# Five batches with the gates' exponential a step sooner and the first scatter a step later, and each following batch's v loaded a pair later

## The chip, the cores and the metric

The kernel runs on one core of one Trainium2 chip. The metric is device time in microseconds (us). The kernel before has a median of 724.61 us over three runs (723.22, 724.61, 727.99).

## The reference

Block-causal attention over q, k and v of shape (8, 8, 576, 64) (batch, head, position, width; blocks of 64 positions), and then a top-1 mixture of eight experts on the 4608 rows of 512 that the attention gives:

```python
scores = scale * np.matmul(q, k.transpose(0, 1, 3, 2))      # masked where block_i < block_j
attn = softmax(scores);  x = np.matmul(attn, v)             # -> (4608, 512)
logits = x @ w_gate;  e_idx = np.argmax(logits, axis=1)
gate_w = softmax(logits)[rows, e_idx]
eom = 1.0 / (1.0 + np.exp(-(x @ w_output_gate)))
out[mask] = gate_w[mask, None] * eom[mask, e, None] * (np.maximum(x[mask] @ w1[e], 0.0) @ w2[e])
```

## The kernel before

The work of the attention goes by batch (8) and by pair of heads (4 in a batch), so there are 32 pairs, p = 0 to 31, b = p // 4. TensorE's (PE's) instructions stand in the order in which the code writes them (`manual_schedule`); on the other engines and on SP's queue a planner sets the order from the order of the code and its own costs, within the edges that `issue_after` adds (`behind()`: after the last chained instruction on POOL; `queued()`: after the last transposing DMA).

`attend` (line 1210 on) writes one pair as a string of letters. For most pairs it is `S.F.SVuFSV.FttSF<t.`; `S` is a step of the softmax of pair p (`softmax`: scores, maximum, exponential, for row tiles 0 and 1, 2, 3, and last the 64 rows that remain), `F` a step that transposes the probabilities of pair p - 1 (`flip`), `V` a half of the values of pair p - 2 (`values`), `t` a step of the generators in `later`, `<` starts `finish_batch`, and a dot calls `others(r)` with r = 0, 1, 2, 3. From p = 26 a pair has four `t`.

`others` prepares inputs. `split_qk` makes 16-bit high and low parts of q and k on POOL (lines 151, 156, 158) for a pair some three ahead. `turn_qk` (line 167) sends one transposing DMA on SP's queue that turns them into the tile `qk` of a pair: 28 of these, for pairs 4 to 31 in order; pairs 0 to 3 are turned on PE. In the first eight pairs it is written at most one pair ahead of its use, later two. `fetch` loads q and k of a later batch (lines 117, 123, 111). `load_v` (lines 336, 338) loads v of the next batch in three DMAs, 512, 512 and 128 KB, one per call of `others`; it starts at the third pair of a batch (`hp == 2`). Tile `vv` has two buffers. `own_keys(b, m)` (line 347) copies parts of v into `vd0` (two buffers) and `vd1` (one) on POOL, which `values` reads from pair 4b on, that is, while p = 4b + 2 is written.

`finish_batch(b)` (line 555 on) starts at the end of p = 4b + 5 and makes the gate's logits, the row numbers and the scatter into the table of rows. For batches 0 to 4 (`slow`) it is cut into some 26 steps of `t`. The steps that matter here: in step 12 the sums of the hot row, `se` and `zs`, on VectorE (DVE, lines 700 to 717); step 13 transposes and scales the last rows of the attention (`part_rows(LAST)`, lines 537, 540); step 14 sends these rows out and has ScalarE (ACT) do the exponential of the gates `zs` (line 724), behind the last softmax exponential written; steps 15 and 16 are small operations on POOL (line 629); step 17 the reciprocal on DVE (line 740); from step 18 on, five scatters on POOL (line 752), two steps apart. The finished rows go to DRAM by SP (line 552).

After the attention come the experts (lines 1128 and 1163), from some 340 us on; nothing there is touched.

Of the kernel before, what the change touches and what calls it, by code (L numbers as in the profile page):

```python
# [26 lines left out]
def block_attention_top1_moe(  # L27
# [12 lines left out]
    B, H, S, D = q.shape  # L40
    NTOK, DM = out.shape
    E, _, FF = w1.shape
    NP = H // 2
# [4 lines left out]
    LAST = NT - 1  # L48
# [92 lines left out]
    def queued():  # L141
        return tc.issue_after(last_turn[0].ins) if last_turn[0] else nullcontext()
# [20 lines left out]
    def turn_qk(p):  # L163

        sp = halves.pop(p)
        qk = sb.tile([P, 2, NB * P], F16, name="qk", bufs=3)
        last_turn[0] = nc.sync.dma_start_transpose(
            qk.rearrange("c h (r n) -> c (h r) n", n=P), sp.rearrange("p h n a d -> p (h n a d)")
        )
        loaded[p] = qk  # L170
# [158 lines left out]
    def load_v(b):  # L329

        vv = sb.tile([P, H, LAST, D], F32, name="vv")
        vd = [None, None]
        vl = vlast[b % 2]
        values_of[b] = vv, vd, vl
        for m in range(2):
            nc.sync.dma_start(vv[:, :, 2 * m:2 * m + 2].rearrange("p h i d -> p h (i d)"), couples(v, b, m))
            yield
        nc.sync.dma_start(vl[0:64], pair_of(v[b, :, S0:S]))
        yield

    def own_keys(b, m):

        vv, vd, vl = values_of[b]
        vd[m] = sb.tile([P, H, D], F32, name=f"vd{m}", bufs=2 - m)
        for i in range(2):
            with behind():
                last_pool[0] = nc.gpsimd.tensor_copy(vd[m][64 * i:64 * i + 64], vv[0:64, :, 2 * m + i])
# [180 lines left out]
    def finish_batch(b, sums, sumL, xT):  # L528
# [3 lines left out]
        def rows(t):  # L532

            r = ROWS[t]
            pm = ps_t.tile([P, 512], F32, name="ps_t")
            for g in range(NP):
                nc.tensor.transpose(pm[0:r, P * g:P * g + P], xT[:, g, Q0[t]:Q0[t] + r], ident)
            xn = sbx.tile([P, DM], F32, name="xn", bufs=NT - 1)
            with tc.high_priority(offset=5):
                last_row[0] = nc.vector.tensor_tensor(  # L540
                    xn[0:r].rearrange("p (h d) -> p h d", d=D), pm[0:r].rearrange("p (h d) -> p h d", d=D),
                    rec[0:r, t].unsqueeze(2).broadcast_to([r, H, D]), ALU.mult,
                )
            held.append((x_d[b * S + Q0[t]:b * S + Q0[t] + r, :], xn[0:r]))
            if rush:
                store()

        def store():

            while held:  # L550
                with queued() if not rush else nullcontext():
                    nc.sync.dma_start(*held.pop())
# [13 lines left out]
        held, rush, mid, slow = [], b == B - 1, b == B - 3, b < B - 3  # L566
# [66 lines left out]
        def after(last):  # L633
            return tc.issue_after(last[0].ins) if pool else nullcontext()

        def part(n):

            for x in range(n if slow else 0):
                yield

        def part_rows(*ts):

            for t in ts:
                rows(t)
                yield
                store()
# [70 lines left out]
            nc.vector.tensor_reduce(zs, z, AX.X, ALU.add)  # L717
        if slow:
            yield
            yield from part_rows(LAST)  # L720
        if mid:
            yield
        with after(last_exp) if pool or rush else tc.issue_after(last_flip[0].ins):
            last_gate[0] = nc.scalar.activation(zs, zs, AF.Exp, scale=-1.0)
        yield from part(1)
        if slow:
            on_pool(
# [10 lines left out]
        yield from part(1)  # L738
        with after(last_max):
            nc.vector.reciprocal(idg.bitcast(F32)[:, b, :, 1], zs)  # L740
        yield from part(1)
        if mid:
            rows(2)
        for t in range(NT):
            r = ROWS[t]
# [261 lines left out]
    def load_first():  # L1007

        route_first()
        for j in range(2):  # L1010
            with behind():
                last_pool[0] = nc.gpsimd.memset(xg[j], 0.0)
        with behind():
            fetch_ids(steps[0])
        fetch_ids(steps[1], (0, 1))
        last_pool[0] = read[0]
        with chain():
            ev = nc.sync.value_load(f_i[0:1, 0:1], min_val=0, max_val=E - 1)

        wc = {}  # L1020

        def load(w, c):
            dt, nm = ((F16, "hh"), (BF16, "hl"))[c % 2]
            wc[c] = fs.tile([P, KF, 2, P], dt, name=nm).rearrange("p f h n -> p (f h n)").bitcast(F32)
            nc.sync.dma_start(quarter(w, wc[c]), rows_of(w, ev, c))

        for c in range(4):
            load(w1, c)
        with behind():
            read[0] = nc.gpsimd.tensor_copy(w1b[0][:, 0, 0], wc[0].rearrange("p (g m) -> p g m", g=KF))  # L1030
        with tc.issue_after(read[0].ins):
            fetch_x(steps[0])
        fetch_x(steps[1], (0, 1))
        for r in range(5):
            yield
        for c in (1, 0, 2, 3):
            if c:
                with tc.issue_after(last_exp[0].ins):
                    nc.scalar.copy(w1b[0][:, 0, c], wc[c].rearrange("p (g m) -> p g m", g=KF))
            for g in range(0, KF, 4):  # L1040
                with tc.issue_after({1: last_max, 0: last_row, 2: last_xT, 3: last_low}[c][0].ins):
                    nc.vector.tensor_tensor(
                        w1b[0][:, 1, c, g:g + 4].bitcast(BF16), wc[c].rearrange("p (g m) -> p g m", g=KF)[:, g:g + 4],
                        w1b[0][:, 0, c, g:g + 4], ALU.subtract,
                    )
            load(w2, c)
            for r in range((1, 3, 1, 0)[c]):
                yield
        first_w2.extend(wc[c] for c in range(4))
# [160 lines left out]
    def step(g, n=1):  # L1210
        for i in range(n):
            next(g, None)
# [45 lines left out]
    for p in range(NPR):  # L1258
        b, hp = divmod(p, NP)
        if hp == 0:  # L1260
            sums = small.tile([P, NT, H], F32, name="sums", bufs=3), small.tile([P, NP], F32, name="sumL", bufs=3)
            nc.gpsimd.memset(sums[0][64:128, LAST, :], 1.0)
            xT = sbx.tile([P, NP, S], F32, name="xT")
        if p == NPR - 2:
            ld.release()
            wp = ctx.enter_context(tc.tile_pool(name="wp", bufs=1, side="right"))
            fs = ctx.enter_context(tc.tile_pool(name="fs", bufs=2, side="right"))
            w1b.append(wp.tile([P, 2, KD, KF, P], F16, name="w1b0"))
            w2b.append(wp.tile([P, 2, KF, DM], F16, name="w2b0"))
            for j in range(2):  # L1270
                xg.append(wp.tile([P, 2, DM], F32, name=f"xg{j}"))
            later.append(load_first())
        if p == 0:
            fetching.append(load_v(0))
        if b + 1 < B and hp == 2:
            fetching.append(load_v(b + 1))
        early = turn_first(p + 1) if p + 1 < NP else None

        def others(r):
            if early is not None:  # L1280
                step(early)
            if r % 2 == 0 and qk_next[0] in halves and qk_next[0] <= p + 1 + (p >= SURE):
                turn_qk(qk_next[0])
                qk_next[0] += 1
            if not splits and splitted[0] < min(NPR, p + 3 + (p >= SURE)):
                splits.append(split_qk(splitted[0]))
                splitted[0] += 1
            for g in list(splits):
                if next(g, splits) is splits:
                    splits.remove(g)  # L1290
            for m in range(2):
                if (p, r) == ((max(1, NP * b), 1), (NP * b + 1, 2))[m]:
                    own_keys(b, m)
            nb = fetched[0] + 1
            free = splitted[0] - len(splits) >= NP * (nb - 1) and p >= NP * (nb - 2) + 1
            if nb < B and not r % 2 and (p == 0 and nb == 1 or (p, r) == (2, 2) and nb == 2 or nb > 2 and free):
                fetching.append(fetch(nb))
                fetched[0] = nb
            with queued():
                for g in list(fetching):  # L1300
                    if next(g, fetching) is fetching:
                        fetching.remove(g)

        probs = {}
        attend(softmax(p, *sums, probs), others)
        flips.append((hp, b, probs, sums, xT, values_of[b]))
        if p == CP:
            with tc.issue_after(last_max[0].ins):
                constants()
# [23 lines left out]
    hp, b, pT, vab, sums, xT = prods.pop()  # L1333
# [155 lines left out]
```

## Time and profile before

| | |
|---|---|
| median of three runs | 724.61 us |
| profiled execution | 724.29 us |
| its span, first to last instruction | 722.7 us |
| PE busy | 695.7 us (96%) |
| DVE, ACT, POOL busy | 540.7, 498.5, 336.6 us |
| DMA queue that SP feeds, share of 16 engines | 70.2% |

A timeline row gives the start and the length of a run of equal instructions, the engine, the line, the operation with its tiles and shapes, the count, and in brackets how long the engine stood idle before it and what ended that. SPq is SP's DMA queue: the length there is that of issuing, not of the transfer. The engine's idle time before an instruction is put down to the releaser that came last by the profile; where that one had long been done, it was another.

### The profile page before, as it was taken

Reading aid. Unit: us, or ns where it says so; the run is one execution under the profiler, and the core shown is the slowest. Engines: PE = TensorE matmul, PEld = TensorE weight load, DVE = VectorE, ACT = ScalarE, POOL = GpSimd, SP = SyncE. Lnnn points to the kernel's source line nnn. Section 1 sums busy time; section 2 is a strip of 40 time slices with the busy share of each in tenths; the row PEclk is TensorE's granted clock in tenths of the full one; section 3 lists DMA queues with packets and bytes.
Section 4 is the critical chain, followed back from the end, with each engine's and each line's share of the span. In section 5 each row is a group of like instructions: output and inputs, shape, how many; then the busy total and the mean of one; then the engine's idle time right before and its main releaser. Section 6 shows DMA issues by size and latency. Waiting matters only on the chain. (4 is left out here: it accounts for less than half of the span.)

```text
span 722.7 us, 21738 instructions
## 1 busy us (share of the span) xinstructions
PE 695.7 (96%) x8604; PEld 508.8 (70%) x8604; DVE 540.7 (75%) x947; ACT 498.5 (69%) x1096; POOL 336.6 (47%) x447
## 2 busy tenths in 40 slices
PE   8999999999999998998999999999999999999994
PEld 6677877777777776677577758677586676757761
DVE  6878988898988896796887658667586687858730
ACT  6889887788888885772476667566675777757630
POOL 4575688778787776315456314222143134211011
PEclk9999999999999999999999999999999999999997
DMA  7999499999899864479376886947999999777611
GB/s 191 273 200 249 94 236 157 211 198 213 175 187 200 158 128 66 162 228 240 88 135 171 262 281 159 265 144 210 301 308 291 333 339 300 261 228 168 241 37 41
DMA packets 218847, 146.88 MB, mean 203 GB/s; under 512 B 153584, under 2 KB 186416, under 8 KB 218736
## 3 DMA queue, kind: packets, MB, share of 16 engines
q1 hardware_dynamic: 209984, 125.85, 70.2%
q0 software_dynamic: 8208, 19.29, 9.3%
q8 instruction: 69, 1.13, 0.7%
q14 instruction: 42, 0.34, 0.2%
q10 hardware_dynamic: 544, 0.26, 0.1%
HBM read 126.43 MB, written 19.34 MB: 202 GB/s over the span
## 5 line engine op out<-in xcount | busy, mean ns | idle before, releaser
L1128 PEld LDWEIGHTS <-w1b 128*128 128x128 f16 (+1 forms) x2208 | 176.7, 98 | 21.9 <-issue 1.7
L1128 PE MATMUL ps_s<-xt,w1b 128*128 128x256 f16 (+5 forms) x1920 | 174.8, 253 | 0.0
L1163 PE MATMUL ps_t<-w2b,hh 128*128 128x512 f16 (+1 forms) x560 | 166.6, 379 | 0.0
L992 DVE TENSOR_TENSOR w2b<-w2f,w2b 128x1024 bf16<-128x1024 f32 x80 | 92.8, 1220 | 87.1 <-ACT w2b L990 85.0
L395 DVE TENSOR_REDUCE nmx<-ps_s 128x1 f32<-128x512 f32 (+4 forms) x224 | 130.0, 616 | 23.2 <-PE ps_s L384 8.9
L388 ACT ACTIVATE pt<-ps_s,nmx 128x256 f32<-128x256 f32 (+3 forms) x256 | 132.2, 532 | 5.9 <-DVE nmx L395 4.6
L1171 POOL DMA_INDIRECT out_dram<-ys,ids x38 | 45.5, 1199 | 169.2 <-ACT ys L1170 85.9
L1163 PE MATMUL ps_t<-w2b,hl 128*128 128x512 f16 x280 | 106.1, 379 | 0.0
L1170 ACT ACTIVATE ys<-ps_t,ids 128x512 f32<-128x512 f32 (+1 forms) x38 | 26.0, 685 | 105.6 <-PE ps_t L1163 76.5
L1163 PEld LDWEIGHTS <-hh 128*128 128x128 f16 x560 | 54.4, 98 | 61.8
L992 DVE TENSOR_TENSOR w1b<-w1f,w1b 128x1024 bf16<-128x1024 f32 x80 | 93.2, 1218 | 5.4 <-ACT w1b L990 5.1
L990 ACT CAST w1b<-w1f 128x1024 f16<-128x1024 f32 x80 | 78.4, 1045 | 8.4 <-DMA w1f<-in_moe_w_dram 8.4
L505 PE MATMUL ps_t<-pT,vv 128*64 128x128 f32 (+1 forms) x512 | 80.1, 392 | 0.0
L990 ACT CAST w2b<-w2f 128x1024 f16<-128x1024 f32 x80 | 77.8, 1043 | 0.9 <-DMA w2f<-in_moe_w_dram 0.8
L375 PE MATMUL ps_s<-qk 64*128 64x256 f16 (+1 forms) x1152 | 72.5, 253 | 4.1 <-ACT pt L388 1.9
L468 DVE COPY pT<-ps_f 128x512 f32<-128x512 f32 x93 | 63.5, 683 | 17.1 <-PE ps_f L465 13.2
L959 POOL DMA_INDIRECT xg<-x_d,ids x38 | 54.8, 1442 | 31.7 <-DVE w1b L992 9.4
L468 ACT COPY pT<-ps_f 128x512 f32<-128x512 f32 x93 | 55.2, 594 | 14.2 <-PE ps_f L465 11.4
L375 PEld LDWEIGHTS <-qk 64*128 64x128 f16 x1152 | 48.4, 95 | 17.0 <-issue 12.0
L752 POOL DMA_INDIRECT tab_d<-idg,sli x40 | 41.4, 1034 | 34.8 <-DVE idg L740 13.6
L465 PEld LDWEIGHTS ps_f<-ident,pt 64*128 64x128 f32 x1116 | 42.3, 138 | 21.3 <-issue 15.3
L1136 ACT ACTIVATE hh<-ps_s 128x1024 f16<-128x1024 f32 (+2 forms) x46 | 38.9, 846 | 26.2 <-PE ps_s L1128 24.1
(228 smaller groups left out, 1113.9 us busy)
## 6 DMA issues: line engine op xcount, KB each, us to landing
w1f<-in_moe_w_dram SPq DMA_DIRECT2D x80, 512.0 KB
w2f<-in_moe_w_dram SPq DMA_DIRECT2D x80, 512.0 KB
vv<-in_v_dram SPq DMA_DIRECT2D x16, 512.0 KB
x_d<-xn SPq DMA_DIRECT2D x32, 256.0 KB
natk<-in_k_dram SPq DMA_DIRECT2D x14, 512.0 KB
natq<-in_q_dram SPq DMA_DIRECT2D x28, 256.0 KB
hh<-in_moe_w_dram SPq DMA_DIRECT2D x4, 512.0 KB
hl<-in_moe_w_dram SPq DMA_DIRECT2D x4, 512.0 KB
```

The source lines that it names most:

```text
L375: nc.tensor.matmul(ps[:, ab, c:c + m], qk[rows, cq, P * t:P * t + P], cols(qk[rows, ck], x, kind), start=(i == 0), stop=(i == 2 and c + m ...
L388: last_exp[0] = nc.scalar.activation(probs[t][:, ab], ps[:, ab, c0:c0 + n], AF.Exp, bias=nmx[:, t, ab:ab + 1], accum_out=sums[:, t, 2 * hp ...
L395: last_max[0] = nc.vector.tensor_reduce(o, x, AX.X, ALU.max, negate=True)
L465: nc.tensor.transpose(ps[:, h, 64 * i:64 * i + 64], src[rows], ident[rows, rows])
L468: copy(to[:, h], ps[:, h].rearrange("p (s c) -> p s c", c=P))
L505: nc.tensor.matmul(pa[o, P * t0:P * t1].rearrange("p (t h n) -> p t h n", h=2, n=64), vd[j // 2][:, a0 + ab] if t1 == j + 1 and j % 2 == 0 ...
L959: nc.gpsimd.indirect_dma_start(out=xg[i % NXG][:, h], out_offset=None, in_=x_d[0:nx, :], in_offset=IOA(ap=ids[i][:, h, 0:1].bitcast(U32), ...
L990: nc.scalar.copy(hi, src)
L992: eng.tensor_tensor(lo, src, hi, ALU.subtract)
L1128: nc.tensor.matmul(ph[:, f4].rearrange("p (h n) -> p h n", n=w), wv[:, cc, f, :], xv[:, cc, :, 0:w], start=(k == 0), stop=(k == 3 * KD - 1))
L1163: nc.tensor.matmul(py, hv[:, f, h], wv[:, f, :], start=(k == 0), stop=(k == 3 * KF - 1))
L1171: nc.gpsimd.indirect_dma_start(out=out, out_offset=IOA(ap=ids[i][0:r, h, 0:1].bitcast(U32), axis=0), in_=ys[0:r], in_offset=None, bounds_c ...
```

## The change

Four edits. In `finish_batch`, for the slow batches, `part_rows(LAST)` moves behind the exponential of the gates, so that the exponential is written in step 13, ahead of the last rows, instead of in step 14. The wait between the reciprocal and the first scatter becomes two steps instead of one for the slow batches, so the five scatters are written a step later each. `load_v(b + 1)` starts at the fourth pair of a batch instead of the third. And `own_keys(b, 0)` is written at p = 4b + 1, r = 0, instead of p = 4b, r = 1, for b > 0.

```diff
@@ finish_batch
         if slow:
             yield
-            yield from part_rows(LAST)
         if mid:
             yield
         with after(last_exp) if pool or rush else tc.issue_after(last_flip[0].ins):
             last_gate[0] = nc.scalar.activation(zs, zs, AF.Exp, scale=-1.0)
+        if slow:
+            yield from part_rows(LAST)
         yield from part(1)
@@
         with after(last_max):
             nc.vector.reciprocal(idg.bitcast(F32)[:, b, :, 1], zs)
-        yield from part(1)
+        yield from part(2)
         if mid:
             rows(2)
@@ the loop over pairs
-        if b + 1 < B and hp == 2:
+        if b + 1 < B and hp == NP - 1:
             fetching.append(load_v(b + 1))
@@ others
             for m in range(2):
-                if (p, r) == ((max(1, NP * b), 1), (NP * b + 1, 2))[m]:
+                if (p, r) == ((NP * b + 1, 0 if b else 1), (NP * b + 1, 2))[m]:
                     own_keys(b, m)
```

## Rows read from the trace of the kernel before

**Rows 1.** The page's part 1, PE's line: busy us, share, instructions.

```profile
PE 695.7 (96%) x8604; PEld 508.8 (70%) x8604; DVE 540.7 (75%) x947; ACT 498.5 (69%) x1096; POOL 336.6 (47%) x447
```

**Rows 2.** Windows: PE, PEld, DVE, ACT, POOL busy (instructions), granted clock, DMA share, GB/s.

```profile
120.00:140.00 20.00, 18.88 (x333) 14.48 (x330) 16.28 (x38) 15.34 (x50) 15.99 (x26) 1.00 1.04 200
160.00:180.00 20.00, 19.97 (x359) 15.32 (x357) 16.72 (x39) 16.76 (x54) 16.25 (x30) 1.00 0.93 204
```

**Rows 3.** Timeline of PE and its weight loads: starts of pairs 5, 13, 14, the values, a transpose.

```profile
49.62 0.34 PE L375 MATMUL ps_s<-qk 64*128 64x128 f16 x6 [0.19 <-ACT pt L388]
122.72 0.34 PE L375 MATMUL ps_s<-qk 64*128 64x128 f16 x6 [1.10 <-ACT d L676]
...
122.72 0.17 PEld L375 LDWEIGHTS <-qk 64*128 64x128 f16 x6 [1.33 <-DMA qk<-sp]
...
132.53 0.34 PE L375 MATMUL ps_s<-qk 64*128 64x128 f16 x5
...
134.93 0.39 PE L505 MATMUL ps_t<-pT,vd 128*64 128x128 f32 x4
...
141.65 0.66 PE L596 MATMUL ps_t<-ident,lgT 128*128 128x128 f32 x4 [0.24 <-ACT lgT L564]
```

**Rows 4.** Timeline of SP's queue, third batch into the fourth.

```profile
98.75 3.02 SPq L336 DMA_DIRECT2D vv<-in_v_dram  x2
...
108.14 0.73 SPq L338 DMA_DIRECT2D vlast<-in_v_dram  x1
...
111.28 3.56 SPq L167 DMA_TRANSPOSE qk<-sp  x1
...
116.99 5.52 SPq L167 DMA_TRANSPOSE qk<-sp  x1
```

**Rows 5.** Timeline of ACT around line 724, two batches, and DVE's reciprocal.

```profile
102.34 0.23 ACT L724 ACTIVATE zs<-zs 128x5 f32<-128x5 f32 x1
102.45 0.60 ACT L564 COPY lgT<-ps_t 128x512 f32<-128x512 f32 x1
...
133.87 0.59 ACT L468 COPY pT<-ps_f 128x512 f32<-128x512 f32 x1 [0.65 <-PE ps_f L465]
...
133.25 0.40 DVE L590 RECIPROCAL rec<-rec 128x40 f32<-128x40 f32 x1 [0.41 <-ACT rec L585]
```

**Rows 6.** Timeline of POOL: copies of v, the gates' steps, a first scatter.

```profile
128.15 1.27 POOL L347 COPY vd<-vv 64x512 f32<-64x512 f32 x2 [0.16 <-PE ps_t L505]
...
141.27 0.23 POOL L629 TENSOR_SCALAR zs<-zs 128x5 f32<-128x5 f32 x1 [3.64 <-ACT zs L724]
...
149.41 1.06 POOL L752 DMA_INDIRECT tab_d<-idg,sli  x1 [2.71 <-DVE xT L523]
```

**Rows 7.** Timeline of SP's queue, first batch into the second.

```profile
26.88 1.25 SPq L336 DMA_DIRECT2D vv<-in_v_dram  x2
28.17 2.42 SPq L338 DMA_DIRECT2D vlast<-in_v_dram  x1
...
41.65 4.11 SPq L167 DMA_TRANSPOSE qk<-sp  x1
```

**Rows 8.** Timeline of PE, POOL and SP around pair 29.

```profile
261.54 0.92 PE L435 MATMUL ps_s<-qk,qlast 128*128 128x256 f16 x9
270.68 0.90 PE L435 MATMUL ps_s<-qk,qlast 128*128 128x256 f16 x9
...
282.48 0.22 PE L519 MATMUL ps_t<-pT,vv 128*64 128x64 f32 x1 [1.63 <-issue]
...
284.24 1.62 PE L435 MATMUL ps_s<-qk,qlast 128*128 128x256 f16 x9
...
270.87 1.27 POOL L347 COPY vd<-vv 64x512 f32<-64x512 f32 x2
...
274.08 2.93 SPq L167 DMA_TRANSPOSE qk<-sp  x1
```

**Rows 9.** Windows around pair 29, columns as in rows 2.

```profile
282.00:288.00 6.00, 5.01 (x67) 3.77 (x66) 3.30 (x6) 3.64 (x9) 3.91 (x5) 0.72 0.01 2
```

## The prediction

> **What bounds it now.** I read the page first, for the share of each engine [rows 1], then windows over the attention to see in which stretches PE is idle [rows 2], then the timeline of PE there [rows 3], and for each gap the queue or engine that ended it [rows 4 to 9]. PE is busy for 695.7 of 722.7 us [rows 1], and no other engine comes near. In an undisturbed stretch of the attention it is idle for 0.03 us in 20; in the stretch from 120 to 140 for 1.12 [rows 2]. So the change, which takes no work off PE, can only win back single gaps. I find three that it touches.
>
> The largest in the regular part of the attention is that of 1.10 us ahead of the first scores of pair 13 at 122.72. The row of PE names ACT, but the weight load of the same step waited 1.33 us for the transposed tile [rows 3]: the transposing DMA of pair 13, the tenth of the 28, issued from 111.28 to 114.84, landed nearly 8 us after its issue ended. Ahead of it on SP's queue stand the three DMAs of v of the batch [rows 4]. The second gap is 0.24 us at 141.65, where PE waits for ACT's copy of the logits [rows 3], and the gates' exponential stands right ahead of that copy on ACT, 0.23 us long [rows 5]. The third is in pair 29: from its predecessor's last softmax step to its own pass 13.56 us, against 9.14 for the pair before that [rows 8].
>
> **The parts.** *v a pair later.* What moves is three issues per batch for seven batches, 3.02 + 0.73 us on SP in the batch shown [rows 4], and 1,152 KB; at the 200 to 204 GB/s of the stretches [rows 2] that is some 5.8 us of the DMA engines. They come to stand behind the transposing DMA that is written in the fourth pair of a batch, instead of ahead of it; in the batch shown that is pair 13's, which so goes out some 3.75 us sooner with 5.8 us less in front; it needs 1.33. Bounds: from 0 (the lateness came from something else in the queue) to 1.33; I take the 1.10 that PE stood idle.
>
> The same v now stands ahead of the next transposing DMA, pair 14's: issued from 116.99 to 122.51 [rows 4], used at 132.53 [rows 3], so 10.0 us are there between the end of the issue and the use. At the 7.9 us that pair 13's took, 2.1 are spare, and an undisturbed queue leaves more. I take 0 for it, since the 7.9 us were seen with v in front and at a DMA share of 1.04 and above, and the shares of the other batches are lower [rows 2]; the other end is in the rivals.
>
> In the first batch the distance is shorter, as a pair's transposing DMA is there written one pair ahead only. Pair 5's is issued from 41.65 to 45.76 [rows 7] and used at 49.62, and PE did not wait for it (its 0.19 us went to ACT) [rows 3]: at most 3.86 us are spare. The v of batch 1, 1.25 + 2.42 us of issue from 26.88 on [rows 7], moves from ahead of pair 4's transposing DMA to between pair 4's and pair 5's. It stood ahead of pair 5's before too, so only what the queue cannot fill in its place is lost. Bounds: 0, if the loads of q and k close the hole, and 5.8 if none of it is filled and nothing was spare; I take 0.3, near the low end, since 3.86 of the 5.8 may be covered.
>
> *The copy of v on POOL.* The same 1.27 us [rows 6], a pair later. Its reader is the value product two pairs into the batch: the second copy, at 128.15 and done at 129.42 [rows 6], stays where it is, the first now stands just before it, and the first product that reads either is at 134.93 [rows 3]. That leaves 5.5 us, so 0. If v had not landed, POOL would stand with the splits of q and k behind it; but from its issue to the copy there are still some two pairs of about 9.14 us [rows 8], against 5.8 of transfer. `vv` has two buffers, and the load comes later than before, so it waits for no release.
>
> *The exponential a step sooner.* It takes 0.23 us of ACT away from ahead of the logits' copy [rows 5], five times: between 0 and 5 x 0.24 = 1.2 us; I take 0.24, since of the five batches one shows PE waiting there. It then stands behind the last softmax exponential one pair earlier, where ACT stood idle for 0.65 us soon after [rows 5], which covers it; but the sums' copy for the next batch comes behind it, and DVE already waits 0.41 us for that ahead of the next maximum [rows 5]. Bounds: 0 to 5 x 0.23 = 1.15; I take 0.2. On POOL the wait of 3.64 us for the exponential goes [rows 6], and what is late next is the first scatter: it waits 2.71 us for DVE's reciprocal (the row names another DVE instruction) [rows 6] and will wait that much longer. POOL's splits come sooner, and PE waits for none of them. So 0.
>
> *The last rows behind it.* The transposes on PE and the scaling stay in the same step and in their order among PE's instructions; their DMA is in step 14 as before. 0.
>
> *The scatters a step later.* Five issues on POOL, about 1.06 us each [rows 6], per slow batch. Nothing before the experts reads the table, POOL is busy for 16 of 20 us [rows 2], and the splits that they are moved past serve pairs two and more ahead: 0, and at most 1.06 us once if a split came to be late.
>
> *Pair 29.* Its PE gap has rows like 1.63 us with "issue" as releaser: PE waited for nothing that the profile shows [rows 8]. Behind it the granted clock is 0.72 over 6 us [rows 9], that is, in part at 1.2 instead of 2.4 GHz, and a softmax step takes 1.62 us instead of 0.90 [rows 8]. Just ahead of it, the transposing DMA of pair 31 leaves at 274.08, when POOL has split its q and k, and the copy of v that the change moves stood in that split for 1.27 us [rows 8]. So that DMA would leave 1.3 us sooner against PE's work. Whether this moves the gap no row tells: the bounds are a gain of 13.56 - 9.14 = 4.4 and 1.7 us of clock (0.28 of 6 us [rows 9]), and a loss of 1.3. I take 0.
>
> **The sum.** 724.29 (the profiled execution, 1.6 us around its span and 0.3 below the median of 724.61) - 1.1 - 0.24 + 0.2 + 0.3 = 723.45, so 723.4 us.
>
> A rule speaks for no gain from moving loads around a transposing DMA. In the rows the DMA share is 0.93 to 1.04 while 200 to 204 GB/s are moved [rows 2]. The Trainium skill (Advanced Engine Details and Errata, X-Bar Transpose (TRN2)) says that transposing DMAs are as fast as regular ones, and gives 350 to 400 GB/s; with so fast a queue nothing would be late behind 1,152 KB, and the time would be the third rival's. The trace does not agree: its engines are taken up at about half that rate.
>
> **Rivals.** *First, the gap of pair 29 goes too* with the earlier transposing DMA: 723.45 - 4.4 - 1.7 = 717.4, and in part anything up to 721.5. For it: the DMA share falls to 0.01 just after [rows 9], so something that was in flight then ended the stall. Against: most of what surrounds it (stores, scatters of a batch that the change leaves alone) stays. Chance 0.2.
>
> *Second, slower: the transposing DMA behind v comes late.* v's 5.8 us beat the 2.1 us that are spare at pair 14's, and so for pairs 10, 18, 22, 26 and 30, and for pair 5. A late one costs up to 3.7 us; priced like the one that the trace shows, 1.10, all seven make 723.15 + 7.7 = 730.9, and half of them 727. It decides where such a DMA lands more than 10.0 us after its issue. For it: DMA shares around 1 [rows 2]. Against: v left the queue ahead of it by as much. Chance 0.13.
>
> *Third, nothing to measure:* pair 13's was late because its own transfer was slow, and stays late, or another takes its place. 724.3 to 725. For it: among 28 only one was waited for, though all batches load v alike. Chance 0.17.
>
> **The numbers.** The forecast, 723.4 with 721.5 to 724.3 of its own, has 0.5. The range of 718.0 to 727.5 leaves out the lower end of the first rival and, of the second, the case that more than half are late. One per cent, about what a measurement of this kernel can tell from no change, is 7.2 us: under 717.4 needs all of the first rival and more (0.07), over 731.9 the second at nearly its worst (0.04), and 0.89 is between.
>
> **What would show it.** Right: the weight load at pair 13 waits for no transposed tile; v's DMAs stand behind the transposing DMA written in the fourth pair of a batch on SP; POOL no longer waits for the gates' exponential, and waits longer for the reciprocal ahead of the first scatter; the step ahead of the logits' transposes is free of waits. Wrong: weight loads wait for transposed tiles at pairs 5, 10, 14, 18, 22; PE is idle for longer around pair 29, or not at all; a new wait of DVE's maximum for ACT at the start of a batch.

## The result, and the profile after

The changed kernel takes 732.45 us in the median of 19 runs (726.18 to 736.45), the kernel before 725.94 us in as many beside it: 1.0091 times as long, 95% interval 1.0071 to 1.0111. Such ratios, here and below, leave out executions in a slower state of the chip (in e2 two of six) and can differ by some tenths of a per cent from the quotient of the medians shown. The forecast was 723.4 us, about 1 us less than before, with a range to 727.5; the change is slower by some 6.5 us, and the time lies outside the range. The profiled execution took 733.86 us, its span is 732.2 against 722.7 us.

Where the 9.5 us of span went is read from the start of the last softmax step (line 435) of each pair, in both timelines:

| stretch | before | after | difference |
|---|---|---|---|
| start to pair 0 | 13.60 | 14.52 | +0.92 |
| pair 5 | 8.07 | 9.61 | +1.54 |
| pair 13 | 10.10 | 8.94 | -1.16 |
| pair 15 | 8.85 | 8.41 | -0.44 |
| pair 18 | 10.13 | 12.83 | +2.70 |
| pair 25 | 8.98 | 10.87 | +1.89 |
| pairs 29 to 31 | 35.49 | 37.76 | +2.27 |
| pair 31 to the end | 416.52 | 418.16 | +1.64 |

The pairs not listed differ by at most 0.53 us each and cancel. The first and the last two rows make 4.83 us, half of it, and do not belong to the kernel alone: e9 below, the changed kernel on another chip, takes 13.47, 28.37 and 415.59 us there.

The windows show the same, PE's share above all. Columns: start and end, length, then busy us (instructions) of PE, PEld, DVE, ACT and POOL, granted clock, DMA share, GB/s.

```profile
40.00:60.00 20.00, 18.21 (x345) 14.52 (x341) 15.29 (x32) 17.08 (x53) 11.17 (x16) 1.00 0.98 224
120.00:140.00 20.00, 19.97 (x364) 16.18 (x363) 17.54 (x41) 16.77 (x55) 17.91 (x26) 1.00 0.99 220
160.00:180.00 20.00, 17.49 (x317) 13.65 (x317) 15.45 (x36) 14.23 (x47) 14.81 (x24) 1.00 1.19 208
```

The two stretches of [rows 2] have changed places: that from 120 to 140 is now free of gaps, as forecast, and that from 160 to 180, which had 0.03 us of idle PE, has 2.51. The page has PE busy for 697.9 of 732.2 us, 2.2 more than in [rows 1], and idle for 7.3 more. Three places of the timeline say why. First pair 5, on PE, its weight load and SP's queue, the answer to [rows 3, 7]:

```profile
52.10 0.34 PE L375 MATMUL ps_s<-qk 64*128 64x128 f16 x6 [1.74 <-DMA qk<-sp]
52.09 0.17 PEld L375 LDWEIGHTS <-qk 64*128 64x128 f16 x6 [1.97 <-DMA qk<-sp]
...
33.36 2.91 SPq L167 DMA_TRANSPOSE qk<-sp  x1
36.94 0.70 SPq L336 DMA_DIRECT2D vv<-in_v_dram  x1
39.42 1.09 SPq L336 DMA_DIRECT2D vv<-in_v_dram  x1
42.04 1.90 SPq L338 DMA_DIRECT2D vlast<-in_v_dram  x1
45.23 3.77 SPq L167 DMA_TRANSPOSE qk<-sp  x1
```

Batch 1's v now stands between the transposing DMAs of pairs 4 and 5. That of pair 5 goes out at 45.23 instead of 41.65 (0.92 of that is the later start), and PE waits 1.74 us for the transposed tile. Second pair 13, the gap that the forecast wanted back, on PE and SP, the answer to [rows 3, 4]:

```profile
124.06 0.34 PE L375 MATMUL ps_s<-qk 64*128 64x128 f16 x6
...
108.90 4.62 SPq L167 DMA_TRANSPOSE qk<-sp  x1
114.95 1.25 SPq L336 DMA_DIRECT2D vv<-in_v_dram  x2
116.24 6.64 SPq L338 DMA_DIRECT2D vlast<-in_v_dram  x1
123.04 4.12 SPq L167 DMA_TRANSPOSE qk<-sp  x1
```

PE does not wait there, and v stands behind the transposing DMA. Third pair 18, the largest loss, on POOL and then on PE:

```profile
164.05 0.72 POOL L156 CAST sp<-natq 128x640 f16<-128x640 f32 x1
168.97 0.72 POOL L156 CAST sp<-natq 128x640 f16<-128x640 f32 x1 [4.20 <-DMA qk<-sp]
...
174.03 0.60 POOL L156 CAST sp<-natk 128x512 f16<-128x512 f32 x1
174.72 1.16 POOL L158 TENSOR_TENSOR sp<-natk,sp 128x512 f16<-128x512 f32 x1
...
177.01 1.29 POOL L347 COPY vd<-vv 64x512 f32<-64x512 f32 x2
...
178.36 0.44 PE L505 MATMUL ps_t<-pT,vd 128*64 128x128 f32 x4 [2.49 <-POOL vd L347]
```

Two casts of q (line 156) follow each other: the splits of two pairs are mixed. The second of them waits 4.20 us until a transposing DMA has let go of a buffer of `sp`, and the second copy of v, which in [rows 6] came right behind one split, now comes behind both. PE waits 2.49 us for it. Nothing in the diff touches that copy: the planner reordered POOL. Splits are mixed so in four places in each of the five traces that have the scatters' edit with POOL's order left to the planner (the change, e2, e9, e10, e15), and in none of the other fifteen. Pair 25 has another gap: PE waits 1.74 us for DVE's scaling of the rows (line 540) at 239.59, and why that is late no row tells.

Pair 29 is as before [rows 8] or worse: its last step starts at 291.87, 15.63 us behind its predecessor's.

```profile
276.24 0.90 PE L435 MATMUL ps_s<-qk,qlast 128*128 128x256 f16 x9
291.87 0.92 PE L435 MATMUL ps_s<-qk,qlast 128*128 128x256 f16 x9
```

### The profile page after: what moved, and what is told of

Its sections match the earlier page's. It is cut to its first block, busy times and chain, and to the rows that moved or that the text cites. A ratio compares the mean times of both kernels' runs of the same rounds, so it can differ in the third digit from the quotient of the medians.

```text
span 732.2 us, 21736 instructions
## 1 busy us (share of the span) xinstructions
PE 697.9 (95%) x8604; PEld 510.1 (70%) x8604; DVE 542.0 (74%) x947; ACT 498.3 (68%) x1096; POOL 334.1 (46%) x447
## 5 line engine op out<-in xcount | busy, mean ns | idle before, releaser
L960 POOL DMA_INDIRECT xg<-x_d,ids x38 | 53.0, 1395 | 34.9 <-DVE w1b L993 10.1
```

Source lines behind the costliest of these rows:

```text
L960: nc.gpsimd.indirect_dma_start(out=xg[i % NXG][:, h], out_offset=None, in_=x_d[0:nx, :], in_offset=IOA(ap=ids[i][:, h, 0:1].bitcast(U32), ...
```

## The experiments

The kernels of one set (a table below, or e17 and e18) ran on one chip, beside the kernel before, whose median differs from chip to chip (717.7 to 729.4 us); so only ratios to it are compared, best within a set. In brackets stands the 95% interval.

Theory 1: the scatters' step makes the planner regroup POOL, and that carries the loss. Theory 2: the loads of v behind the transposing DMA carry it.

### The edits one by one

Each kernel has one of the four edits of the diff and nothing else.

> Only the first edit: the gates' exponential of the slow batches stands ahead of the last rows. Theory 1 (the scatters' step regroups POOL's splits and pushes the second copy of v back): within 2 us of the kernel before, as POOL's order stays. Rival (the exponential in its new place on ACT holds up the sums' copy and the next maximum): 4 to 8 us slower, with ACT and DVE waits at the start of pairs 9, 13, 17, 21, 25.

> Only the second edit: part(2) in place of part(1) ahead of the scatters. Theory 1: this edit alone carries the loss, 4 to 7 us slower than before, with the splits of two pairs interleaved on POOL in the second pair of a slow batch, the second copy of v some 10 us later there, and weight loads that wait for vd or for transposed tiles. Theory 2 (the loads of v behind the transposing DMA carry it): within 1 us of before.

> Only the third edit: v of the next batch loaded in the last pair of a batch. Theory 1: no slower than before, and 0 to 1 us faster, with pair 13's transposed tile in time and pair 5's late by some 1.7 us. Theory 2: 4 to 7 us slower, with transposed tiles late in several pairs.

> Only the fourth edit: the first copy of v written a pair later on POOL, behind the next pair's scale. Theory 1: within 1 us of before. Rival (the later copy holds up the splits behind it, or v's reader): 3 to 7 us slower with PE waiting for vd in the second pair of a batch.

| | median us | to before (720.24) |
|---|---|---|
| e1, exponential | 721.4 | 1.0012 [0.9981, 1.0043] |
| e2, scatters | 735.48 | 1.0144 [1.0087, 1.0201] |
| e3, load of v | 724.47 | 1.0051 [1.0015, 1.0087] |
| e4, copy of v | 717.28 | 0.9958 [0.9930, 0.9987] |

The scatters' edit alone costs more than the whole change did, though the intervals overlap. Its trace has PE waiting for the second copy again (1.09 us in pair 14), and for a transposed tile (3.41 us in pair 17), but its largest loss has another mechanism; POOL, DVE and PE in pair 13:

```profile
121.59 0.62 POOL L151 TENSOR_SCALAR natq<-natq 128x512 f32<-128x512 f32 x1 [8.09 <-DMA natq<-in_q_dram]
125.55 0.29 POOL L151 TENSOR_SCALAR natq<-natq 64x128 f32<-64x128 f32 x1 [3.34 <-DMA natq<-in_q_dram]
125.82 0.25 POOL L629 TENSOR_TENSOR d<-L,mx 128x40 f32<-128x40 f32 x1
...
126.86 0.20 DVE L663 TENSOR_REDUCE er<-eq 128x5 f32<-128x40 f32 x1 [6.90 <-POOL eq L629]
126.98 0.21 DVE L523 COPY xT<-ps_t 128x64 f32<-128x64 f32 x1
...
127.24 0.69 PE L490 MATMUL ps_t<-ident,pt 128*128 128x128 f32 x2 [5.78 <-DVE xT L523]
```

The planner put the scaling of the next q (line 151) ahead of the gates' step `d` (line 629). The scaling waits 8.09 and 3.34 us for its load, `d` stands behind it, DVE's maximum `er` waits 6.90 us for POOL, the copy of `xT` stands behind that on DVE, and PE waits 5.78 us for the copy. Before, `d` stood first (113.33, without a wait) and the scaling behind it (114.34). Late loads so stop two engines that have no use for them. The Trainium skill (PSUM — Partial Sum Buffer, Engine vs sequencer instructions) calls the queues of ACT, DVE and POOL strictly first in, first out; this trace agrees, with the 3.34 us that POOL idled ahead of a step that does not read q.

In e3 the first copy of v, not moved, waits up to 7.46 us on POOL for the later load (154.83 to 162.29), but that is not what PE waits for. PE waits for two transposed tiles, those of pairs 17 and 22, and not for that of pair 5, which was expected late; SP and PE of e3:

```profile
153.75 3.07 SPq L167 DMA_TRANSPOSE qk<-sp  x1
156.88 1.47 SPq L336 DMA_DIRECT2D vv<-in_v_dram  x2
...
195.56 7.62 SPq L167 DMA_TRANSPOSE qk<-sp  x1
...
50.57 0.34 PE L375 MATMUL ps_s<-qk 64*128 64x128 f16 x6 [0.19 <-ACT pt L388]
...
160.79 0.50 PE L375 MATMUL ps_s<-qk 64*128 64x128 f16 x6 [2.36 <-DMA qk<-sp]
...
209.45 0.23 PE L375 MATMUL ps_s<-qk 64*128 64x128 f16 x1 [2.62 <-DMA qk<-sp]
```

Pair 17's split was done at 140.63 and its DMA issued from 153.75, before the copy began to wait; v was issued right behind it, at 156.88. Pair 22's DMA stands right behind v on SP (192.53 to 195.40), took 7.62 us to issue, and its tile came 6.3 us after that: the second rival's case. So the late tiles of e3 speak for theory 2. Whether POOL's wait costs anything beside them, and so whether the later copy is needed with the later load, is not shown. Both theories hold in part, theory 1 for the larger share.

### POOL's order held

From e2 it is not plain whether the order is at fault or the scatters' places. In e5 and e7 each chained instruction behind a scatter also gets an edge to the instruction ahead of that scatter; splits, gate steps and copies then stand as before.

```
+            before_sc = last_pool[0]
             with behind():
                 last_pool[0] = nc.gpsimd.indirect_dma_start(
...
+            chain_more[0] = before_sc     # behind() adds an edge to it, once
```

> The second edit alone, as in e2, but with POOL's order held: each chained instruction behind a scatter also gets an edge to the instruction ahead of that scatter. The scatters stand a step later; the splits, gate steps and copies of v stand in the order of before. Theory 1 (the regrouping of POOL's queue is the loss, not the later scatters): within 0.3% of before, no wait of DVE for eq over 1 us. Rival (scatters a step later cost by themselves, by their place or what they delay): 1.0 to 1.4% slower, as e2.

> All but the second edit. Theory 1: 0.1 to 0.5% faster than before, as e4, since the later first copy of v takes away the 7.5 us that POOL waited for v in e3; what stays is pair 5's transposed tile, some 1.5 us late. Rival (the loads of v behind the transposing DMA cost by themselves): 0.3 to 0.6% slower, with transposed tiles late in pairs 13, 17, 21, 22.

> All four edits, with POOL's order held as in e5. Theory 1: as e6 within 0.2%, and 0.5 to 1.2% faster than the changed kernel. Rival: as the changed kernel, 0.9% slower than before.

> The first and the fourth edit alone. If the edits add up as measured alone (+0.1% and -0.4%): 0.2 to 0.4% faster than before. If e6 comes out slower than this by more than 0.2%, the later load of v costs something even where the copy waits for nothing.

| | median us | to before (727.77) |
|---|---|---|
| e5, scatters, order held | 734.74 | 1.0093 [1.0059, 1.0128] |
| e6, all but scatters | 733.25 | 1.0096 [1.0063, 1.0129] |
| e7, all, order held | 736.5 | 1.0123 [1.0084, 1.0162] |
| e8, exponential and copy | 730.28 | 1.0051 [1.0024, 1.0078] |

Theory 1 fails here as it was put: e5 is slow with the order held, and e7 is no faster than the change was. e6, expected 0.1 to 0.5% faster than before, is 0.96% slower; in its trace the one wait of PE for a tile is pair 5's, 1.80 us. And e8 is 0.5% slower than before, though neither of its parts was in the first set: at this size the edits' costs differ from chip to chip, or from one combination to another. In e5 the waits of e2 are gone, and yet pair 14 takes 15.71 us against 10.13 in e4, more than half of the difference by the clock (an estimate: 0.28 of 12 us is 3.4); windows of e5, columns as above:

```profile
124.00:130.00 6.00, 5.97 (x108) 4.86 (x104) 5.07 (x13) 5.71 (x19) 5.60 (x8) 1.00 0.81 127
130.00:142.00 12.00, 9.34 (x110) 6.46 (x109) 6.18 (x14) 5.48 (x19) 8.40 (x13) 0.72 0.99 214
```

DVE's scaling of the rows waits 2.47 us there with a releaser that the profile calls remote, and PE 2.35 us for DVE; behind it the mean granted clock is 0.72, so PE ran in part at 1.2 instead of 2.4 GHz. What held both is not told.

### One edit left out, on one chip

> The changed kernel itself again, on the chip of e10 to e12, for the edits to be told apart on one chip: 0.7 to 1.1% slower than before if what makes it slower belongs to the kernel, and the same stalls as in its first profile (pair 5's transposed tile, the second copy of v in pair 18). If the place of the stalls is chance, other pairs.

> All but the third edit: v loaded in the third pair of a batch as before. If the load behind the transposing DMA costs 0.45 to 0.5% (e3 against before, e6 against e8): 0.4 to 0.5% faster than e9, with pair 5's tile in time. If the scatters' step carries all: as e9.

> All but the second edit, the kernel of e6, on this chip. If the scatters' step adds to the others: 0.2 to 0.6% faster than e9, without the wait for the second copy of v in pair 18. If e6 holds, still 0.4 to 1.0% slower than before.

> The fourth edit alone, the kernel of e4, on this chip: 0.1 to 0.7% faster than before if e4's gain belongs to the kernel; no faster, or slower as e8, if it belonged to the chip.

| | median us | to before (717.7) |
|---|---|---|
| e9, the changed kernel | 721.43 | 1.0058 [1.0027, 1.0088] |
| e10, all but the load | 727.13 | 1.0159 [1.0108, 1.0210] |
| e11, all but the scatters | 718.19 | 1.0010 [0.9979, 1.0042] |
| e12, copy | 717.44 | 0.9987 [0.9962, 1.0012] |

Two expectations missed (e9 came out just under its own, 0.7 to 1.1%). e10 was to be faster than e9 and is 1.0% slower: with v ahead of the transposing DMA, the load that POOL's scaling needs is late again, as in e2. POOL, DVE and PE of e10 in pair 13, and the window from the end of POOL's wait on:

```profile
123.61 0.29 POOL L151 TENSOR_SCALAR natq<-natq 64x128 f32<-64x128 f32 x1 [9.30 <-DMA natq<-in_q_dram]
123.87 0.25 POOL L629 TENSOR_TENSOR d<-L,mx 128x40 f32<-128x40 f32 x1
...
124.92 0.20 DVE L663 TENSOR_REDUCE er<-eq 128x5 f32<-128x40 f32 x1 [6.22 <-POOL eq L629]
...
125.31 0.69 PE L490 MATMUL ps_t<-ident,pt 128*128 128x128 f32 x2 [5.10 <-DVE xT L523]
...
123.50:130.50 7.00, 4.69 (x52) 3.59 (x52) 4.47 (x9) 2.09 (x6) 6.33 (x11) 0.51 0.29 79
```

So the edits are not a sum: the later load, a loss by itself (e3), here saves 1.0%. The scaling stands ahead of `d` in e9 too, but waits 2.62 us there, and 0.38 in the first profile of the change. Why the load lands so late in e10 is not shown: it was issued at 114.31, in e9 at 114.88, and from 121 to 123 the core's DMA engines moved 44 GB/s. And e11 is level with before, where e6, the same kernel, was 0.96% slower on another chip. With the scatters' edit on top of the other three, e9 is 0.48% slower than e11 (the intervals overlap), and its trace repeats what pair 18 showed; PE in pairs 14 and 22:

```profile
142.11 0.44 PE L505 MATMUL ps_t<-pT,vd 128*64 128x128 f32 x4 [0.61 <-POOL vd L347]
...
217.52 0.44 PE L505 MATMUL ps_t<-pT,vd 128*64 128x128 f32 x4 [1.18 <-POOL vd L347]
```

### The first batch's v, and the order once more

e14 is the change without the scatters' edit, and batch 1's v loaded as before; e15 adds the scatters' edit, e16 that with the order held.

```
-        if b + 1 < B and hp == NP - 1:
+        if b + 1 < B and hp == (NP - 1 if b else 2):
```

> All but the second edit, the kernel of e6 and e11, as the partner of e14 on this chip: pair 5's transposed tile late by 1.5 to 5 us, else as before; -0.2 to +0.9% against before, by the chip.

> As e13, but batch 1's v is loaded in the third pair as before, and only the v of batches 2 to 7 a pair later. If the later v costs through pair 5 alone: pair 5's period back at 8.07 us and 0.2 to 0.6% faster than e13. If the other pairs carry it: as e13.

> As e14 with the second edit added, POOL's order left to the planner. If the scatters' step costs by the late second copy of v: 0.3 to 0.6% slower than e14, with PE waiting for vd in pairs 14, 18, 22. If it costs only together with v ahead of the transposing DMA: as e14.

> As e15 with POOL's order held: only the scatters themselves stand a step later. If the order carries the cost: as e14 within 0.2%, and faster than e15. If the places of the scatters do: as e15 or slower, with PE idle beside two scatters in a row.

| | median us | to before (729.44) |
|---|---|---|
| e13, all but the scatters | 734.17 | 1.0038 [1.0005, 1.0070] |
| e14, first v early | 729.46 | 0.9991 [0.9967, 1.0015] |
| e15, with the scatters | 733.25 | 1.0064 [1.0032, 1.0096] |
| e16, order held | 731.89 | 1.0034 [1.0003, 1.0066] |

e13 and then e14, the first scores of pair 5 on PE:

```profile
53.04 0.34 PE L375 MATMUL ps_s<-qk 64*128 64x128 f16 x6 [2.71 <-DMA qk<-sp]
```

```profile
49.66 0.34 PE L375 MATMUL ps_s<-qk 64*128 64x128 f16 x6 [0.19 <-ACT pt L388]
```

PE waited for that tile in all six traces with the later load in every batch and the later copy, for 1.74, 1.80, 3.40, 2.55, 3.57 and 2.71 us (the change, e6, e7, e9, e11, e13); in e14 to e16 and e18 it did not. But e13 also waited 3.88 us for pair 18's tile, the second rival's case, so the 0.47% between e13 and e14, whose intervals just overlap, need not be pair 5 alone. In e3, which has the later load without the later copy, PE did not wait for pair 5's tile (its row at 50.57 above): what the copy adds there is not shown.

e15 has the late second copy in pairs 14, 18, 22 and 26, and e16 in none. e15, PE in these pairs:

```profile
139.30 0.44 PE L505 MATMUL ps_t<-pT,vd 128*64 128x128 f32 x4 [0.99 <-POOL vd L347]
...
177.63 0.44 PE L505 MATMUL ps_t<-pT,vd 128*64 128x128 f32 x4 [0.54 <-POOL vd L347]
...
215.57 0.44 PE L505 MATMUL ps_t<-pT,vd 128*64 128x128 f32 x4 [0.77 <-POOL vd L347]
...
255.66 0.44 PE L505 MATMUL ps_t<-pT,vd 128*64 128x128 f32 x4 [1.45 <-POOL vd L347]
```

The four waits are 3.75 us, 0.5% of the time; e15 is 0.73% slower than e14. In e16 the copy stands at 127.80 instead of 137.96, and the waits are gone, but it is still 0.43% slower than e14; its interval overlaps with that of either. But the four pairs together take 44.83 us in e14, 46.07 in e15 and 45.82 in e16, and the three profiled executions took 730.23, 729.93 and 729.26 us: these traces do not hold the difference that the medians show. In pairs 14 and 18 of e16, not in 22 and 26, eight matmuls of the logits take 1.1 us longer; e14 and then e16, pair 14:

```profile
138.67 1.06 PE L558 MATMUL ps_t<-xT,wg_bd 128*32 128x512 f32 x8
```

```profile
137.85 2.20 PE L566 MATMUL ps_t<-xT,wg_bd 128*32 128x512 f32 x8
```

No row names what held these. So the late copy is shown as a mechanism of the change, and that the order is all of the scatters' cost is not; the scatters' places have a part that stays open. Scatters left out altogether were not tried.

### What remains to gain

> The fourth edit alone a third time (0.42% faster in e4, 0.13% in e12): 0.1 to 0.4% faster than before if the gain belongs to the kernel; if the edit is worth nothing, within 0.2%.

> The fourth edit with the later v from batch 2 on, that is e14 without the first edit, the candidate that the runs leave: as e17 within 0.2% if the later v is worth nothing where no transposed tile comes late; 0.2% or more faster than e17 if the transposing DMAs that go out sooner save stalls.

e17 took 717.73 us, 0.9979 [0.9947, 1.0011] of before (718.97), and e18 715.97 us, 0.9955 [0.9923, 0.9986]. The later copy alone came out at 0.9958, 0.9987 and 0.9979 in three sets; e18, which adds the later v from batch 2 on, was run in one set only. The two are the best versions found, 0.1 to 0.45% below the kernel before; which of them is better their intervals do not tell. Why the copy gains was not tried; it takes 1.27 us of POOL out of a split that a transposing DMA waits for.

## Why the prediction was wrong

**The step that failed** is "The scatters a step later. Five issues on POOL [...] 0, and at most 1.06 us once if a split came to be late", with its companion in the step on the copy of v, "the second copy [...] stays where it is". Both costed the moved scatters in an order of POOL that was taken as given. That order is the planner's answer to the code, and it changed: a scaling of q moved ahead of the gates' step, two splits were mixed, the second copy went behind both. The runs show 10.4 us for this edit alone (1.44% of 720.24, interval 0.87 to 2.01), and 0.48% and 0.73% on top of the others (e9 to e11, whose intervals overlap, and e15 to e14). How much of that is the order and how much the scatters' places stays open: with the order held the edit still costs 0.93% alone (e5, on another chip).

**Pair 5** was in the sum with 0.3 us, between bounds of 0 and 5.8. The place was right and the size wrong: waits of 1.74 to 3.57 us. Of 3.86 us to spare nothing was left; the queue did not fill the hole, as SP issued nothing from 27.41 to 33.36, where v had stood. That this is all of it is not shown, since e3 has v in the same place without the wait.

**Pair 13's gap** went, but it was no property of the kernel before. e1 and e5 leave SP's order through that stretch as it was, with v ahead, and pair 13 takes 8.99 and 9.19 us there against 10.10 in the profile before. Nearest to that was the third rival, with 0.17, which put the lateness down to that one transfer; one gap in one execution had been read as a term that comes back in every run.

**The exponential** was right: POOL no longer waits for it (the row of [rows 6] at 141.27 is now at 140.56 without a wait), the first scatter behind it now waits 4.16 us instead of 2.71, as foreseen; the logits' transposes of [rows 3] are at 142.58 and wait for nothing (another, at 219.60, waits 0.34), and e1 is 0.12% slower than before, which its interval does not tell from nothing. **The later copy** was put at 0; it gains 0.1 to 0.4%, and two of its three intervals include no gain. **Pair 29** did not move in the direction of the first rival. The second rival had the right sign, and late tiles right behind v did come, at pair 22 in e3 (2.62 us) and pair 18 in e13 (3.88), but in the two traces of the changed kernel only at pair 5; the scatters' loss was none of the rivals.

## What to carry to other kernels

Where a planner sets the order of an in-order engine, a moved step has no cost that can be read from the old trace until the new order is laid beside the old one: first ask which waits now stand in front of whom. An instruction that waits for a DMA should not stand ahead of work that another engine's next step needs. And a gap seen once in a profile is a term of a sum only when a second execution has it too.

## What was not expected of the hardware

An idle PE can be paid for twice: in e10 PE stood idle for 5.10 us to 125.31, from 123.5 on the mean granted clock was 0.51 over 7.0 us, nearly all of it at 1.2 instead of 2.4 GHz, and pair 13 took 16.95 us against 8.99 in e11. It is not always: behind the 2.49 us of pair 18 in the changed kernel the clock stayed at 1.00, and the pair took 2.70 us more than before.

And what a stretch costs can belong to the chip: pairs 29 to 31, where the kernel before has its largest gap, take 28.4 to 31.8 us together in the ten traces from chips on which the kernel before has a median of 718 to 720 us (e1 to e4, e9 to e12, e17, e18), and 34.9 to 39.1 us in the ten others, whichever edits they have. No row names what holds PE there.
